# Windowed attention, low-rank mixing and a two-layer network in one kernel: mixing in 64-row halves, and one batch's attention two slots later

## The chip, the cores and the metric

The kernel runs on one core of a Trainium2 chip. The metric is device time in microseconds (us) of a whole execution, lower is better. A core has TensorE (matmuls, with a weight load before each), VectorE, ScalarE and GpSimd, and SyncE, which here only issues transfers. "DMA" is a transfer by the core's DMA engines. PSUM is the memory that matmuls write, divided into banks; SBUF is the other on-chip memory. The granted clock is the share of its full clock that TensorE was allowed, as the profile records it.

## The reference, cut to what matters

```python
# 8 batches, 8 heads, 576 positions, 64 values per head
scores = q @ k.T / sqrt(64)            # causal, window of 64
x = softmax(scores) @ v                # laid out as [batch, 576, 512]
h = (x.T @ U @ V).T                    # U: 576 x 32, V: 32 x 576: mixing along positions
u = x + h
out = u + relu(u @ w_ch1) @ w_ch2      # 512 -> 2048 -> 512
```

The 8 x 576 = 4608 rows are 36 tiles of 128. The network works in nine chunks of four tiles. A batch is four and a half tiles, so batch 3 covers tiles 13 (half of it) to 17, and chunk 3 (tiles 12 to 15) needs the first three of those.

## The kernel before

Everything is placed by hand. Chunk c of the network is 32 "fills" of four 128x512 matmuls each: 16 fills of the first layer (`psA`), then 16 of the second (`psU`, four for each tile). After fill s, the work listed for slot s is put into the program: in chunk c that is attention and mixing of batch c+1. In these traces each engine takes its matmuls, additions or transfers in program order, so "slot" fixes both when work runs and what it stands behind.

```python
PLACE = {"S": [0, 0, 0, 3, 3],   # scores
         "M": [0, 1, 2, 4, 5],   # masks
         "PV": [8],              # probabilities times values -> x
         "U": [14],              # down-product x.T @ U
         "V": [16, 17, 18],      # up-product, and u = x + h
         "UT": [17, 17, 18, 18, 19]}   # transposes of u
PLACE_3 = {**PLACE, "SV": [5, 5, 6, 6]}
...
for fill, extra in zip(mlp(c) + [lambda: None], slots):
    fill()
    for f in extra:
        f()
```

The down-product keeps four partial sums, one for each of the first four row tiles, in four groups of 32 PSUM partitions; the fifth tile is added to all four, 128 columns to each. The up-product contracts all 128 rows with V repeated four times:

```python
def UM(ts):                                  # down-product
    ...
        if t < 4:
            nc.tensor.matmul(hh["ps"][t * R : (t + 1) * R, :], ub[odd][:, t, :], xt,
                             start=True, stop=False)
            continue
        for g in range(4):
            cols = slice(g * P, (g + 1) * P)
            nc.tensor.matmul(hh["ps"][g * R : (g + 1) * R, cols], ub[odd][:, t, :],
                             xt[:, cols], start=False, stop=True)
    ...
def VM(ts):                                  # up-product and addition
    ...
        for n, t in enumerate(ts):
            off = t * P + (0 if odd else W)
            nc.tensor.matmul(ps[0][:, n, :], vrep[:, off : off + P], hh["sb"][:],
                             start=True, stop=True)
    ...                                      # add(n): u = psv + x, on VectorE
def UT(t):
    ...
        if b >= NXT:                         # batches 3 to 7: transposed by DMA
            nc.sync.dma_start_transpose(out=dst, in_=u_tiles[g][:])
            return
```

The last fill of each tile adds u and stores the result, through the same SyncE that issues the transposes:

```python
def ch2(t, quarter, ...):
    ...
        osb = out_pool.tile([P, DM], FP32, name="osb")
        nc.vector.tensor_tensor(out=osb[...], in0=acc[t][...], in1=u_tiles[g][...], op=ALU.add)
        nc.sync.dma_start(out=outf[...], in_=osb[...])
```

So tile 0 of a chunk is stored within slot 19's fill.

The softmax here doesn't subtract the row's maximum and nothing guards it: scores larger than these inputs give would overflow.

Of the kernel before, what the change touches and what calls it, by code (L numbers as in the profile page):

```python
# [12 lines left out]
FP32 = mybir.dt.float32  # L13
# [3 lines left out]
def kernel(  # L17
# [11 lines left out]
    nc = tc.nc  # L29
    B, H, S, D = q.shape  # L30
    DM = H * D
    R = moe_U.shape[1]
    F = moe_w_ch1.shape[1]
    P = nc.NUM_PARTITIONS
    W = 64
# [11 lines left out]
    CH = 512  # L47
# [17 lines left out]
    ps_big = ctx.enter_context(tc.tile_pool(name="ps_big", bufs=2, space=bass.MemoryType.PSUM))  # L65
    ps_tp = ctx.enter_context(tc.tile_pool(name="ps_tp", bufs=1, space=bass.MemoryType.PSUM))
    first = ExitStack()
    psum = {
        "spare": first.enter_context(tc.tile_pool(name="ps_s0", bufs=1, space=bass.MemoryType.PSUM)),
        "mm": first.enter_context(tc.tile_pool(name="ps_t0", bufs=2, space=bass.MemoryType.PSUM)),  # L70
    }
# [9 lines left out]
    NT = 5  # L81
    uf = [const.tile([P, NT, R], FP32, name=f"uf{i}") for i in range(2)]
    ub = [const.tile([P, NT, R], BF16, name=f"ub{i}") for i in range(2)]
    vrep = const.tile([P, W + S + W], BF16, name="vrep")
# [62 lines left out]
    def shift_low(b, copy, t):  # L147
# [9 lines left out]
        out=ident[:],  # L157
# [11 lines left out]
    for n, base, step, mult in ((0, 0, 1, -1), (1, -1, -1, 1), (1, W, 1, -1)):  # L169
        nc.gpsimd.affine_select(  # L170
            out=maskA[:, 0, n, :],
# [18 lines left out]
    for i in range(2):  # L190
# [5 lines left out]
        out=uf[0][:, 0:NFULL, :], in_=moe_U[0 : NFULL * P, :].rearrange("(c p) r -> p c r", p=P)  # L196
# [43 lines left out]
    u_tiles = {}  # L240
    uT_tiles = {}

    def uT_of(c):
        if c not in uT_tiles:
            uT_tiles[c] = uT_pool.tile([P, TPC, NDC, P], BF16, name="uTc")
        return uT_tiles[c]


    def attention(b, spare=False):
        crossbar = b >= NXB  # L250
        odd = b % 2
        kb, qb = staged(b)
        va, vb = vA[odd], vB[odd]
        x = xs[odd]
        g0 = (b * S) // P
        pcs = {}
# [231 lines left out]
        hh = {}  # L488
        xc = lambda src, t, dc: src[:, t, :, :].rearrange("p h d -> p (h d)")[:, dc * P : (dc + 1) * P]

        def UM(ts):
            def f():
                if ts[0] == 0:
                    if spare:
                        hh["ps"] = psum["spare"].tile([P, CH], FP32, name="psh", tag="spare")
                    else:
                        hh["ps"] = ps_big.tile([P, 2, CH], FP32, name="pshh", tag="big")[:, 0, :]
                for t in ts:
                    xt = x[:, t, :, :].rearrange("p h d -> p (h d)")
                    if t < 4:  # L500
                        nc.tensor.matmul(  # L501
                            hh["ps"][t * R : (t + 1) * R, :], ub[odd][:, t, :], xt,
                            start=True, stop=False,
                        )
                        continue

                    for g in range(4):
                        cols = slice(g * P, (g + 1) * P)
                        nc.tensor.matmul(
                            hh["ps"][g * R : (g + 1) * R, cols], ub[odd][:, t, :], xt[:, cols],  # L510
                            start=False, stop=True,
                        )
                if ts[-1] == NT - 1:
                    hh["sb"] = wk_pool.tile([P, CH], BF16, name="hh", tag="hh")
                    for cs in (slice(0, CH // 2), slice(CH // 2, CH)) if spare else (slice(0, CH),):
                        nc.scalar.copy(out=hh["sb"][:, cs], in_=hh["ps"][:, cs])
            return f
# [5 lines left out]
        def bank(dc):  # L523
            if dc not in ua:
                if dc < 2:
                    ua[dc] = psum["mm"].tile([P, CH], FP32, name="uam", tag="mm")[:]
                elif dc == 2:
                    ua[dc] = ps_tp.tile([P, CH], FP32, name="uat", tag="tp")[:]
                else:
                    ua[dc] = ps_big.tile([P, 2, CH], FP32, name="uab", tag="big")[:, 0, :]  # L530
            return ua[dc]
# [15 lines left out]
        def XT(t, dcs):  # L547
            def f():
                opened.append(t)
                for dc in dcs:  # L550
                    cols = bank(dc)[:, t * P : (t + 1) * P]

                    nc.tensor.matmul(cols, xc(x, t, dc), ident[:], start=(t == 0), stop=False)
            return f

        def HT(dcs):
            def f():
                for dc in dcs:
                    nc.tensor.matmul(
                        bank(dc),  # L560
                        hh["sb"][:, dc * P : (dc + 1) * P],
                        vrep[:, W : W + CH],
                        start=False,
                        stop=True,
                    )
                for dc in dcs:
                    copy = nc.scalar.copy if dc % 2 == 0 else nc.vector.tensor_copy
                    copy(
                        out=uT_of(b)[:, :, dc, :],
                        in_=bank(dc).rearrange("p (t q) -> p t q", q=P),  # L570
                    )
            return f

        def VM(ts):
            ps = {}

            def up():
                ps[0] = ps_big.tile([P, 2, CH], FP32, name="psv", tag="big")
                for n, t in enumerate(ts):
                    off = t * P + (0 if odd else W)  # L580
                    nc.tensor.matmul(  # L581
                        ps[0][:, n, :], vrep[:, off : off + P], hh["sb"][:], start=True, stop=True
                    )

            def add(n):
                def f():
                    t = ts[n]
                    g = g0 + t
                    rs = slice(
                        W if (odd and t == 0) else 0, W if (not odd and t == NT - 1) else P  # L590
                    )
                    if g not in u_tiles:
                        u_tiles[g] = u_pool.tile([P, DM], BF16, name="un")
                    nc.vector.tensor_tensor(  # L594
                        out=u_tiles[g][rs, :],
                        in0=ps[0][rs, n, :],
                        in1=x[rs, t, :, :].rearrange("p h d -> p (h d)"),
                        op=ALU.add,
                    )
                return f  # L600

            return [up] + [add(n) for n in range(len(ts))]

        def UT(t):
            def f():
                g = g0 + t
                dst = uT_of(g // TPC)[:, g % TPC, :, :]
                if b >= NXT:
                    nc.sync.dma_start_transpose(out=dst, in_=u_tiles[g][:])
                    return  # L610
                tp = ps_tp.tile([P, NDC, P], BF16, name="tpu", tag="tp")
                for dc in range(NDC):
                    nc.tensor.transpose(  # L613
                        tp[:, dc, :], u_tiles[g][:, dc * P : (dc + 1) * P], ident[:]
                    )
                nc.scalar.copy(out=dst, in_=tp[:])  # L616
            return f
# [13 lines left out]
        if spare:  # L631
            pcs["XT"] = [XT(t, range(NDC - 1)) for t in range(NFULL)]
            pcs["idle"] = idle_turns
            pcs["X3"] = [XT(t, (NDC - 1,)) for t in range(NFULL)]
            pcs["HT"] = [HT((0, 1)), HT((2, 3))]
            pcs["V"] = [f for ts in ((0, 1), (2, 3), (4,)) for f in VM(ts)]
        else:
            def whole(ts):
                fs = VM(ts)
                return lambda: [f() for f in fs]  # L640

            pcs["V"] = [whole(ts) for ts in ((0, 1), (2, 3), (4,))]
            pcs["UT"] = [UT(t) for t in range(NT if odd else NT - 1)]
        return pcs

# [4 lines left out]
    def mlp(c):  # L650
# [65 lines left out]
    PLACE = {  # L716
        "S": [0, 0, 0, 3, 3],
        "M": [0, 1, 2, 4, 5],
        "PV": [8],
        "U": [14],  # L720
        "V": [16, 17, 18],
        "UT": [17, 17, 18, 18, 19],
    }
    PLACE_0 = {"V": [0, 0, 1, 2, 2, 3, 4, 4]}
    PLACE_1 = {
        "T": [11, 11, 12, 12, 14, 14, 15, 15],
        "S": [12, 13, 15, 16, 16],
# [1 line left out]
        "SV": [17, 17, 18, 18],  # L729
        "PV": [19],  # L730
        "U": [24],
        "V": [25, 26, 27],
        "UT": [27, 28, 29, 30, 102],
    }
    PLACE_2 = {
# [2 lines left out]
        "SV": [15, 15, 16, 16],  # L738
        "PV": [18],
        "U": [23],  # L740
        "V": [24, 25, 26],
        "UT": [27, 28, 29, 30],
    }
    PLACE_3 = {**PLACE, "SV": [5, 5, 6, 6]}
    CROSS = {
        0: {2: [16, 17, 18, 19, 20]},
        1: {3: [13, 14, 15, 16, 17], 4: [26, 27, 28, 29, 30]},
# [7 lines left out]
    def turn_over(n, cols, rows=P):  # L755
# [5 lines left out]

    turn_over(62, 96)
    att = {0: attention(0, spare=True)}
    a = att[0]
    nc.vector.tensor_scalar(
        out=maskA[:, 0, 2, :],
        in0=maskA[:, 0, 1, :],
# [6 lines left out]
        out=maskB[:, 0:3, :],  # L774
        in0=maskA[:, 0, 0:3, :],
# [52 lines left out]
    for c in range(NCH):  # L828
# [10 lines left out]
        if b < B:  # L839
# [17 lines left out]
            if 2 < b and b + 2 < B:  # L857
                loads(b, 2)
            where = {1: PLACE_1, 2: PLACE_2, 3: PLACE_3}.get(b, PLACE)
            if b < NXB:  # L860
                place(b, ("T",), where)
            if b == 1:
                place(0, ("V",), PLACE_0)
                slots[6].append(lambda: nc.scalar.copy(out=ub[1][:], in_=uf[1][:]))
# [57 lines left out]
```

## Time and profile before

314.01 us, median of 3 runs (313.83 to 314.18).

The profiled execution was a separate one and took 315.07 us, 1 us more than the median.

| what | number | where read |
|---|---|---|
| span, TensorE busy | 313.4 us, 306.1 us | the page |
| start to start of 128x512 matmuls | 0.216 us | timeline |
| a middle chunk | 32.10 us | scores of batch 4 at 127.42, of batch 5 at 159.52 |
| wait before batch 3's scores | 1.07 us | timeline |
| third transpose of batch 3 landed, and was used | 126.24, 126.47 us | trace, timeline |

First the page: busy time of each engine with its share, then in 40 slices of the span the tenths that TensorE was busy and its granted clock in tenths.

```profile
...
PE 306.1 (98%) x2875; PEld 150.9 (48%) x2875; DVE 162.2 (52%) x298; ACT 108.6 (35%) x174; POOL 101.3 (32%) x133
...
PE   8899999999998999999999999999999999999996
...
PEclk9999999999999999999999999999999999999999
...
```

TensorE is busy in practically every slice at full clock. "Busy" alone would not prove that it is the limit, because reported ends of matmuls are modelled (0.379 us for one, though one starts every 0.216). The chain of waits does: each line is a start, a length and what the end of the kernel was waiting for in that stretch.

```profile
...
89.60 5.37 DMA qf<-qr
...
95.11 0.19 PE low L340
...
99.17 4.42 PE psA L663 x20
...
115.41 11.22 PE psU L687 x52
126.63 0.86 PE psA L663 x4
...
137.20 5.29 PE psA L663 x24
...
```

The transfer in the first line is the one that matters: TensorE waited for its end. The timeline of TensorE at this place (start, length, line, names, shapes, count, and in brackets the idle time before and what ended it):

```profile
...
93.08 1.03 PE L663 MATMUL psA<-uTc,w1b 128*128 128x512 bf16 x4
95.11 0.19 PE L340 MATMUL low<-qf,kf 64*64 64x64 bf16 x1 [1.00 <-DMA qf<-qr]
...
```

The fourth of those `psA` matmuls starts at 93.73, the score matmul 1.383 us later. In other chunks the same step takes 0.309 us, so 1.07 us are lost. The transposed queries landed at 94.98.

The queue of SyncE with VectorE and the mixing, where batch 3's u tiles are made (chunk 2):

```profile
...
112.44 0.59 PE L581 MATMUL psv<-hh,vrep 128*128 128x512 bf16 x2
...
113.07 3.21 DVE L594 TENSOR_TENSOR un<-psv,xs 64x512 bf16<-64x512 f32 x5 [3.88 <-PE psv L581]
...
114.19 0.53 SPq L703 DMA_DIRECT2D out_dram<-osb  x1
...
114.82 6.63 SPq L609 DMA_TRANSPOSE uTc<-un  x4
...
116.31 0.69 DVE L697 TENSOR_TENSOR osb<-psU,un 128x512 f32<-128x512 f32 x1
...
```

The transposes (`uTc<-un`) issue from 114.82 on; the third of them was issued at 117.54 and landed at 126.24. The store of tile 0, whose addition is the `osb` line at 116.31, comes after them. TensorE then goes into chunk 3 without a wait (no bracket at its first `psA`):

```profile
...
123.66 2.97 PE L687 MATMUL psU<-w2b,c 128*128 128x512 bf16 x13
...
126.47 1.03 PE L663 MATMUL psA<-uTc,w1b 128*128 128x512 bf16 x4
...
```

### The profile page before, as it was taken

How to read it: one execution, taken by the hardware profiler on the slowest of the kernel's cores; microseconds unless marked ns; L12 is line 12 of the kernel's file. 1: busy time of each engine (PE TensorE's matmuls, PEld its weight loads, DVE VectorE, ACT ScalarE, POOL GpSimd, SP SyncE). 2: the span in 40 equal slices, each digit the busy share in tenths (PEclk: the TensorE clock that was granted, in tenths of full speed). 3: DMA queues.
4: the chain of work that ended last, by engine and by line, in shares of the span. 5: the costliest groups of instructions: out<-in, count | busy, mean ns of one | idle time of the engine just before them, and what ended most of it. 6: DMA issues, size and time to landing. Idle time of an engine off the chain costs nothing.

```text
span 313.4 us, 6904 instructions
## 1 busy us (share of the span) xinstructions
PE 306.1 (98%) x2875; PEld 150.9 (48%) x2875; DVE 162.2 (52%) x298; ACT 108.6 (35%) x174; POOL 101.3 (32%) x133
## 2 busy tenths in 40 slices
PE   8899999999998999999999999999999999999996
PEld 7554554544444544454445444544454444444443
DVE  4475468337756843684358445744574443016011
ACT  3655660467027520533043404440345003301500
POOL 8683263159439346426543571000000000000000
PEclk9999999999999999999999999999999999999999
DMA  7999999999999999999999999965100520020012
GB/s 104 164 208 208 206 168 146 129 180 192 121 153 200 159 152 147 193 140 159 175 174 156 170 156 158 178 99 131 67 2 2 134 84 2 14 86 33 2 61 73
DMA packets 156495, 39.87 MB, mean 127 GB/s; under 512 B 145040, under 2 KB 151440, under 8 KB 156464
## 3 DMA queue, kind: packets, MB, share of 16 engines
q0 software_dynamic: 104720, 18.88, 82.5%
q1 hardware_dynamic: 51744, 20.55, 39.2%
q8 instruction: 22, 0.36, 0.4%
q14 instruction: 9, 0.07, 0.1%
HBM read 37.97 MB, written 9.44 MB: 151 GB/s over the span
## 4 chain that ended last, share of the span: by engine, by line
PE 81%; DMA 13%; POOL 3%; DVE 2%; issue 1%; SPq 0%; POOLq 0%
PE psU L687 36%; PE psA L663 36%; DMA qr<-in_q_dram 4%; DMA vB<-in_v_dram 4%; DMA vA<-in_v_dram 3%; PE psv L581 2%; PE xw L402 2%; PE sc L340 2%; DMA qf<-qr 2%; DVE xs L469 1%; POOL vA L134 1%; PE pshh L501 1%; POOL kr L116 1%; PE tpu L613 0%; POOL vrep L220 0%
## 5 line engine op out<-in xcount | busy, mean ns | idle before, releaser
L687 PE MATMUL psU<-w2b,c 128*128 128x512 bf16 (+2 forms) x592 | 131.3, 373 | 0.1
L663 PE MATMUL psA<-uTc,w1b 128*128 128x512 bf16 x576 | 131.0, 379 | 0.0
L687 PEld LDWEIGHTS <-c 128*128 128x128 bf16 x592 | 56.6, 98 | 64.8 <-issue 0.5
L663 PEld LDWEIGHTS <-w1b 128*128 128x128 bf16 x576 | 54.2, 98 | 64.4 <-issue 1.8
L675 ACT ACTIVATE c<-psA 128x512 bf16<-128x512 f32 x84 | 50.1, 597 | 88.8 <-PE psA L663 88.2
L697 DVE TENSOR_TENSOR osb<-psU,un 128x512 f32<-128x512 f32 (+2 forms) x37 | 24.9, 677 | 76.7 <-PE psU L687 76.3
L673 DVE TENSOR_SCALAR c<-psA 128x512 bf16<-128x512 f32 x60 | 41.3, 689 | 25.5 <-PE psA L663 25.5
L594 DVE TENSOR_TENSOR un<-psv,xs 128x512 bf16<-128x512 f32 (+1 forms) x40 | 25.5, 685 | 22.9 <-PE psv L581 22.7
L134 POOL DMA_DIRECT2D vA<-in_v_dram x32 | 28.6, 909 | 17.3 <-PE psU L687 3.1
L360 ACT ACTIVATE pts<-sc 128x1024 bf16<-128x1024 f32 x32 | 31.3, 1028 | 2.7 <-PE sc L340 2.7
L125 POOL DMA_DIRECT2D kr<-in_k_dram x30 | 25.8, 860 | 10.1 <-DMA vA<-in_v_dram 3.5
L125 POOL DMA_DIRECT2D qr<-in_q_dram x30 | 25.9, 864 | 8.9 <-DMA w2b<-in_moe_w_ch_dram 3.2
L393 ACT ACTIVATE ptl<-low 128x256 bf16<-128x256 f32 x6 | 2.3, 384 | 64.4 <-PE high L340 64.4
L366 DVE TENSOR_TENSOR pts<-pts,maskA 128x1024 bf16<-128x1024 bf16 x28 | 19.1, 682 | 1.1 <-ACT pts L360 1.1
L469 DVE TENSOR_TENSOR xs<-xw,rcw 128x896 bf16<-128x896 f32 x14 | 15.3, 1092 | 0.5
L340 PEld LDWEIGHTS <-kf 64*64 64x64 bf16 x704 | 9.9, 107 | 8.8 <-issue 8.2
L846 POOL COPY held<-qf 1x1 bf16<-1x1 bf16 x6 | 1.1, 178 | 39.4 <-DMA qf<-qr 39.4
L581 PE MATMUL psv<-hh,vrep 128*128 128x512 bf16 x40 | 12.5, 379 | 0.0
L402 PEld LDWEIGHTS <-pts 128*64 128x64 bf16 x512 | 10.0, 110 | 4.7 <-issue 3.7
L340 PE MATMUL sc<-qf,kf 64*64 64x128 bf16 (+1 forms) x608 | 11.6, 212 | 0.6 <-DVE qf L293 0.6
L134 POOL DMA_DIRECT2D vB<-in_v_dram x8 | 7.2, 901 | 5.9 <-DMA qr<-in_q_dram 2.5
L616 ACT COPY uTc<-tpu 128x512 bf16<-128x512 bf16 x9 | 5.3, 586 | 10.8 <-PE tpu L613 10.8
(108 smaller groups left out, 171.2 us busy)
## 6 DMA issues: line engine op xcount, KB each, us to landing
out_dram<-osb SPq DMA_DIRECT2D x35, 256.0 KB, 5.0
vA<-in_v_dram POOLq DMA_DIRECT2D x32, 128.0 KB, 13.1
kr<-in_k_dram POOLq DMA_DIRECT2D x24, 128.0 KB, 8.7
qr<-in_q_dram POOLq DMA_DIRECT2D x24, 128.0 KB, 8.9
w2b<-in_moe_w_ch_dram POOLq DMA_DIRECT2D x4, 512.0 KB, 15.7
vB<-in_v_dram POOLq DMA_DIRECT2D x8, 128.0 KB, 13.7
w1b<-in_moe_w_ch_dram POOLq DMA_DIRECT2D x2, 512.0 KB, 10.9
w1b<-in_moe_w_ch_dram POOLq DMA_DIRECT2D x1, 1024.0 KB, 10.0
```

Source lines behind the costliest of these rows:

```text
L125: nc.gpsimd.dma_start(out=dst[0:rows, t, :, :], in_=src[b, :, t * P : t * P + rows, :].rearrange("h p d -> p h d"),)
L134: nc.gpsimd.dma_start(out=dst[:, :, 0:D], in_=v[b, :, lo : lo + P, :].rearrange("h p d -> p h d"))
L340: nc.tensor.matmul(sc[g][r0 : r0 + W, col * W : (col + n) * W], keys_of(j, u, rs), queries_of(j, blk, n, rs), start=not spare, stop=last o ...
L360: nc.scalar.activation(out=dst, in_=sc[:], func=ACT.Exp, scale=scale)
L366: nc.vector.tensor_tensor(out=dst, in0=dst, in1=maskA.rearrange("p g n w -> p g (n w)"), op=ALU.mult)
L581: nc.tensor.matmul(ps[0][:, n, :], vrep[:, off : off + P], hh["sb"][:], start=True, stop=True)
L594: nc.vector.tensor_tensor(out=u_tiles[g][rs, :], in0=ps[0][rs, n, :], in1=x[rs, t, :, :].rearrange("p h d -> p (h d)"), op=ALU.add,)
L663: nc.tensor.matmul(ps[i][:], w1b[:, dc, i * P : (i + 1) * P], uTc[:, :, dc, :], start=(dc == 0), stop=(dc == NDC - 1),)
L673: nc.vector.tensor_relu(out=c1[i][:], in_=ps[i][:])
L675: nc.scalar.activation(out=c1[i][:], in_=ps[i][:], func=ACT.Relu)
L687: nc.tensor.matmul(acc[t][:, lo:hi], c1[i][:, t * P : (t + 1) * P], w2b[:, i, lo:hi], start=(i == 0), stop=(i == NFC - 1),)
L697: nc.vector.tensor_tensor(out=osb[:, lo:hi], in0=acc[t][:, lo:hi], in1=u_tiles[g][:, lo:hi], op=ALU.add,)
```

## The change: its intent and its diff

Two partial sums instead of four let the up-product contract 64 rows, so that two of its matmuls fit on the array side by side and run together. The price is that each row tile of the down-product is multiplied into two groups. All up-products of a batch move into one slot, with two more PSUM banks borrowed for the fifth tile. Batch 3's part of chunk 2 moves two slots later, to cover the wait for its queries.

```diff
 # down-product
-                        nc.tensor.matmul(
-                            hh["ps"][t * R : (t + 1) * R, :], ub[odd][:, t, :], xt,
-                            start=True, stop=False,
-                        )
+                        for g in (t % 2, t % 2 + 2):
+                            nc.tensor.matmul(
+                                hh["ps"][g * R : (g + 1) * R, :], ub[odd][:, t, :], xt,
+                                start=(t < 2), stop=False,
+                            )
...
-                        cols = slice(g * P, (g + 1) * P)
+                        cols = slice((g % 2) * CH // 2, (g % 2 + 1) * CH // 2)
 # up-product; HT, the first one of batch 0, is halved in the same way
-                for n, t in enumerate(ts):
-                    off = t * P + (0 if odd else W)
+                for n in range(2):
+                    half = slice(n * 2 * R, (n + 1) * 2 * R)
+                    off = ts[n % len(ts)] * P + (0 if odd else W)
+                    lo = 0 if len(ts) == 2 else n * cols
                     nc.tensor.matmul(
-                        ps[0][:, n, :], vrep[:, off : off + P], hh["sb"][:], start=True, stop=True
+                        ps[0][n], vrep[half, off : off + P], hh["sb"][half, lo : lo + cols],
+                        start=True, stop=True,
                     )
...
+            def mixed():
+                parts = [VM((0, 1)), VM((2, 3)), VM((NT - 1,), two_banks)]
+                for part in parts:
+                    part[0]()
+                for part in parts[2:] + parts[:2]:
+                    for add in part[1:]:
+                        add()
...
-        "V": [16, 17, 18],
+        "V": [16],
...
-    PLACE_3 = {**PLACE, "SV": [5, 5, 6, 6]}
+    PLACE_3 = {part: [s + 2 for s in at] for part, at in PLACE.items()}
+    PLACE_3["SV"] = [7, 7, 8, 8]
```

With "+2", batch 3's up-product stands at slot 18 and its transposes at 19, 19, 20, 20, 21.

More of the change, by code (lines that the diff above doesn't have):

```diff
@@ L557, in f @@
             def f():
-                for dc in dcs:
+                for n, dc in enumerate(dcs):
+                    half = slice(n * 2 * R, (n + 1) * 2 * R)
                     nc.tensor.matmul(
                         bank(dc),
-                        hh["sb"][:, dc * P : (dc + 1) * P],
-                        vrep[:, W : W + CH],
+                        hh["sb"][half, dc * P : (dc + 1) * P],
+                        vrep[half, W : W + CH],
                         start=False,
@@ L572, in HT, with VM @@
             return f
-        def VM(ts):
+        def VM(ts, banks=None):
             ps = {}
+            cols = CH if len(ts) == 2 else CH // 2
             def up():
-                ps[0] = ps_big.tile([P, 2, CH], FP32, name="psv", tag="big")
-                for n, t in enumerate(ts):
-                    off = t * P + (0 if odd else W)
+                if banks is None:
+                    pair = ps_big.tile([P, 2, CH], FP32, name="psv", tag="big")
+                    ps[0] = [pair[:, n, 0:cols] for n in range(2)]
+                else:
+                    ps[0] = [one[:, 0:cols] for one in banks()]
+                for n in range(2):
+                    half = slice(n * 2 * R, (n + 1) * 2 * R)
+                    off = ts[n % len(ts)] * P + (0 if odd else W)
+                    lo = 0 if len(ts) == 2 else n * cols
                     nc.tensor.matmul(
-                        ps[0][:, n, :], vrep[:, off : off + P], hh["sb"][:], start=True, stop=True
+                        ps[0][n], vrep[half, off : off + P], hh["sb"][half, lo : lo + cols],
+                        start=True, stop=True,
                     )
@@ L586, in f @@
                 def f():
-                    t = ts[n]
+                    t = ts[n % len(ts)]
                     g = g0 + t
@@ L591, in f @@
                     )
+                    cs = slice(0, CH) if len(ts) == 2 else slice(n * cols, (n + 1) * cols)
                     if g not in u_tiles:
@@ L594, in f @@
                     nc.vector.tensor_tensor(
-                        out=u_tiles[g][rs, :],
-                        in0=ps[0][rs, n, :],
-                        in1=x[rs, t, :, :].rearrange("p h d -> p (h d)"),
+                        out=u_tiles[g][rs, cs],
+                        in0=ps[0][n][rs],
+                        in1=x[rs, t, :, :].rearrange("p h d -> p (h d)")[:, cs],
                         op=ALU.add,
@@ L600, in add @@
                 return f
-            return [up] + [add(n) for n in range(len(ts))]
+            return [up, add(0), add(1)]
         def UT(t):
@@ L637, in attention, with two_banks @@
         else:
-            def whole(ts):
-                fs = VM(ts)
-                return lambda: [f() for f in fs]
-            pcs["V"] = [whole(ts) for ts in ((0, 1), (2, 3), (4,))]
+            def two_banks():
+                return (
+                    psum["mm"].tile([P, CH], FP32, name="psv0", tag="mm"),
+                    ps_tp.tile([P, CH], FP32, name="psv1", tag="tp"),
+                )
+            def mixed():
[5 more added lines that the diff above has]
+                        add()
+            pcs["V"] = [mixed]
             pcs["UT"] = [UT(t) for t in range(NT if odd else NT - 1)]
@@ L720 @@
         "U": [14],
-        "V": [16, 17, 18],
+        "V": [16],
         "UT": [17, 17, 18, 18, 19],
     }
-    PLACE_0 = {"V": [0, 0, 1, 2, 2, 3, 4, 4]}
+    PLACE_0 = {"V": [0, 0, 1, 2, 2, 3, 4, 4, 4]}
     PLACE_1 = {
@@ L731 @@
         "U": [24],
-        "V": [25, 26, 27],
+        "V": [25],
         "UT": [27, 28, 29, 30, 102],
@@ L740 @@
         "U": [23],
-        "V": [24, 25, 26],
+        "V": [24],
         "UT": [27, 28, 29, 30],
     }
-    PLACE_3 = {**PLACE, "SV": [5, 5, 6, 6]}
+    PLACE_3 = {part: [s + 2 for s in at] for part, at in PLACE.items()}
+    PLACE_3["SV"] = [7, 7, 8, 8]
     CROSS = {
```

## The prediction

> **What bounds it.** TensorE: the page gives it 306.1 of 313.4 us busy at full clock, and from 130 us on the chain of waits is TensorE almost without a break. In the timeline 128x512 matmuls start every 0.216 us; a middle chunk repeats every 32.10 us (127.49, 159.59). The one sizeable idle stretch after the start is at 95.11 us: batch 3's first score matmul waits for transposed queries (landed 94.98). It starts 1.383 us after the matmul before it; elsewhere that step takes 0.309, so 1.07 us are lost.
>
> **What the change does to TensorE**, from start-to-start times:
> - Up-product now: five matmuls, 5 x 0.216 = 1.08 us per batch, no cost at their edges. After: two pairs of 64-row halves of 512 columns and one of 256. If a pair runs concurrently (the Trainium skill, "TensorE: Matmul & The Clock Gate", Part 3, says that matmuls on different row groups do; in this trace the four 32-column matmuls of the down-product start 3 ns apart), that is 0.54 us. But partial-array blocks pay at their edges here: 0.309 instead of 0.216 on entry, about 0.10 more on exit. Estimate 0.74: saves 0.34.
> - Down-product: each row tile goes to two column groups, so two rounds of 0.216 instead of one, and the last tile streams 256 columns, not 128: +0.27.
> - Net about -0.07 per batch, -0.5 us in all; in batch 0 nothing, as copies follow its first up-product.
> - Two slots (1.73 us) cover batch 3's 1.07 us wait; perhaps 0.15 returns, because ScalarE's exponentials now precede a ReLU.
>
> **What it breaks.** Chunk 3's first matmul needs batch 3's first three u tiles, transposed by DMA. Now the third is issued at 117.54 and lands at 126.24; that matmul starts at 126.47: 0.2 us of slack. After, batch 3's mixing stands at slot 18, at about T = 113.3 us; its own 0.74 and 13 fills of 0.863 bring TensorE to chunk 3 at T+12.0 = 125.3. The transposes come later: all six additions are one run on VectorE (estimate: end T+4.25), and slot 19's output store now precedes them in the DMA queue, waiting for an addition behind that run (T+4.9). So they issue at about T+5.6, 6.9, 8.3, and the third lands, with 7.7 us as measured around 122, near 129.3. TensorE would wait about 4 us (1.5 to 5.5). Such a wait may also lower the clock (same page, Part 1; no run here shows it yet). Other chunks need only two tiles, placed ahead of the store: no wait.
>
> **Sum**: 314.0 - 0.5 - 1.07 + 0.15 + 4 = 316.6; allowing for a shorter or missing wait, 316.0 us, range 312.2 to 318.6. Chances: faster by over 2% 0.01, within 2% 0.95, slower by over 2% 0.04.
>
> **What would show it.** (1) Psv pairs starting a few ns apart, the block about 0.74 us. (2) The pshh block 0.27 us longer. (3) No DMA wait before batch 3's scores. (4) A TensorE wait of about 4 us on uTc at the first psA of chunk 3, near 125 us, and an output store ahead of the uTc transposes in the DMA queue. (5) Middle chunks near 32.03 us.
>
> **What would make it wrong.** Halves that do not overlap (+0.5 us per batch). Transposes landing faster, or issued before the store: then about 312.5. Clock loss after the wait: 318 or more. PSUM banks borrowed for the last part delaying the next chunk.

## The result, and the profile after

318.62 us, median of 6 runs (316.16 to 319.34), against 314.1 us (313.63 to 314.52) in the same rounds. The ratio is 1.013, 95% interval 1.0092 to 1.0168: slower, but by less than 2%. Ratios here and below are the mean time of one kernel's runs over that of the other's in the same rounds, so not quite the ratio of the medians.

The page after:

```profile
...
PE 306.5 (97%) x2915; PEld 148.7 (47%) x2915; DVE 162.7 (51%) x306; ACT 109.1 (34%) x174; POOL 101.2 (32%) x133
...
PE   8889999999999998799999999999999999999996
...
PEclk9999999999999999799999999999999999999999
...
```

In the sixteenth and seventeenth slices (118.7 to 134.5 us) TensorE is no longer full, and in the second of them its clock is at 0.7. The chain of waits shows what stands before it:

```profile
...
113.11 0.69 PE psv L590 x6
...
114.13 0.41 DVE un L605
...
115.27 1.89 DVE un L605 x3
117.15 0.61 DVE osb L718
117.78 0.34 SPq L724
118.16 1.30 SPq L620
119.52 1.43 SPq L620
120.99 7.08 DMA uTc<-un
128.21 1.31 PE psA L684 x4
...
```

Read downwards: up-product of batch 3 (113.11), its six additions (to 117.15), the addition for tile 0's output (117.15), its store (SPq, the queue of SyncE, 117.78), the transposes of u (118.16, 119.52), the third one's landing (120.99 to 128.08), and only then the first `psA` of chunk 3. The same stretch in the timeline, as shown for the kernel before:

```profile
...
113.04 0.71 PE L590 MATMUL psv<-hh,vrep 64*128 64x512 bf16 x6
...
113.79 3.36 DVE L605 TENSOR_TENSOR un<-psv,xs 128x256 bf16<-128x256 f32 x6 [4.36 <-PE psv L590]
113.83 4.29 SPq L724 DMA_DIRECT2D out_dram<-osb  x2
...
117.07 0.68 DVE L718 TENSOR_TENSOR osb<-psU,un 128x512 f32<-128x512 f32 x1
...
118.16 4.15 SPq L620 DMA_TRANSPOSE uTc<-un  x3
...
```

The store line at 113.83 merges two: that of chunk 1's last tile, and the one that waited for the addition at 117.07. Before, three of the transposes had been issued by 118.9. TensorE at the start of chunk 3:

```profile
...
123.63 1.46 PE L708 MATMUL psU<-w2b,c 128*128 128x512 bf16 x6
128.21 1.31 PE L684 MATMUL psA<-uTc,w1b 128*128 128x512 bf16 x4 [3.13 <-DMA uTc<-un]
...
```

From start to start, 3.505 us lie between the last `psU` and this `psA` instead of 0.216: a wait of 3.29 us. The wait before batch 3's scores is gone: they start 0.309 us after the matmul before them.

The wait is not all. Busy time of each engine, its instructions, the granted clock (third number from the end), DMA share and GB/s in three stretches: chunk 2, 3 and 4 of the changed kernel, each from its first `psA` to the next chunk's.

```profile
...
92.88:128.21 35.33, 32.21 (x307) 14.90 (x306) 20.73 (x37) 11.85 (x19) 20.99 (x26) 1.00 1.86 166
128.21:161.79 33.58, 33.58 (x306) 15.61 (x307) 17.91 (x32) 10.28 (x16) 15.23 (x19) 0.95 1.81 165
161.79:193.84 32.05, 32.05 (x308) 14.99 (x307) 18.55 (x33) 10.28 (x16) 12.92 (x16) 1.00 1.92 171
...
```

Chunk 3 takes 33.58 us and chunk 4, with the same work, 32.05. In chunk 3 four `psA` matmuls still start 0.215 to 0.244 us apart after the wait; then the clock falls to a half (0.50 from 128.85 to 132.20): the score matmuls that follow are slowed too, the next `psA`, from 130.66 to 132.29, start 0.37 to 0.43 us apart, and after that 0.216 again. Chunk 3 loses 1.5 us to it (33.58 less 32.05).

The mixing itself, for batch 4, before and after:

```profile
...
142.41 0.40 PE L501 MATMUL pshh<-xs,ub 128*32 128x512 bf16 x4
...
144.54 0.59 PE L581 MATMUL psv<-hh,vrep 128*128 128x512 bf16 x2
...
```

```profile
...
145.69 0.61 PE L502 MATMUL pshh<-xs,ub 128*32 128x512 bf16 x8
...
148.18 0.71 PE L590 MATMUL psv<-hh,vrep 64*128 64x512 bf16 x6
...
```

The six matmuls of the new up-product start in pairs 3 to 4 ns apart. From the last matmul on the full array to the next such one, less one ordinary step, the block takes 0.742 us instead of five steps of 0.216 (1.08). The down-product takes 0.75 instead of 0.48. A middle chunk takes 32.04 or 32.05 us instead of 32.10.

Where the profiled executions differ (spans of 316.43 and 313.37 us), from the starts of the chunks' first `psA`:

| stretch | before | after | difference |
|---|---|---|---|
| to the first psA | 21.97 | 22.41 | +0.44 |
| chunk 0 | 37.89 | 37.31 | -0.58 |
| chunk 1 | 33.22 | 33.16 | -0.06 |
| chunk 2 | 33.39 | 35.33 | +1.94 |
| chunk 3 | 32.10 | 33.58 | +1.48 |
| the rest | 154.80 | 154.64 | -0.16 |

Of the first line, 0.38 us is the arrival of the first queries, which differs from execution to execution. Of chunk 0, about 0.5 us is a wait for batch 1's values that this execution of the kernel before had and another one with the same mixing (e2 below, 37.41 us) had not. Chunk 2 is 3.29 of new wait, 1.07 of vanished wait, 0.2 that is lost no more in batch 3's values product and what follows it (from its first matmul to the down-product 6.79 us before, 6.58 after), and 0.07 of mixing.

The two profiles are 3.06 us apart, the times 4.1 (by the ratio) to 4.5 us (by the medians). The profiled execution of the kernel before was 1 us slower than its median, and three of the six of the changed kernel took 319.09 to 319.34 us, about 1 us more than its profiled one (318.14 us). Those three were not traced, so where their further microsecond went is not known.

### The profile page after: what moved, and what is told of

Read it like the earlier page. It is cut to its first block, busy times and chain, and to the rows that moved or that the text cites. A ratio compares the mean times of both kernels' runs of the same rounds, so it can differ in the third digit from the quotient of the medians.

```text
span 316.4 us, 6992 instructions
## 1 busy us (share of the span) xinstructions
PE 306.5 (97%) x2915; PEld 148.7 (47%) x2915; DVE 162.7 (51%) x306; ACT 109.1 (34%) x174; POOL 101.2 (32%) x133
## 4 chain that ended last, share of the span: by engine, by line
PE 90%; DMA 4%; DVE 2%; SPq 1%; ACT 1%; issue 1%; POOL 0%; POOLq 0%
PE psA L684 41%; PE psU L708 36%; PE sc L340 3%; PE xw L402 2%; DMA uTc<-un 2%; DMA qr<-in_q_dram 2%; PE psv L590 2%; PE pshh L502 1%; SPq L620 1%; DVE un L605 1%; PE tpu L624 1%; ACT pts L360 1%; PE tpg L276 1%; PE xr L402 1%; DVE qf L293 0%
## 5 line engine op out<-in xcount | busy, mean ns | idle before, releaser
L708 PE MATMUL psU<-w2b,c 128*128 128x512 bf16 (+2 forms) x592 | 129.4, 374 | 0.0
L708 PEld LDWEIGHTS <-c 128*128 128x128 bf16 x592 | 55.9, 98 | 65.5 <-issue 3.2
L605 DVE TENSOR_TENSOR un<-psv,xs 128x512 bf16<-128x512 f32 (+3 forms) x48 | 26.1, 592 | 26.0 <-PE psv L590 25.8
L517 ACT CAST hh<-pshh 128x512 bf16<-128x512 f32 x7 | 4.1, 585 | 13.6 <-PE pshh L510 13.5
```

The source lines that it names most:

```text
L605: nc.vector.tensor_tensor(out=u_tiles[g][rs, cs], in0=ps[0][n][rs], in1=x[rs, t, :, :].rearrange("p h d -> p (h d)")[:, cs], op=ALU.add,)
L708: nc.tensor.matmul(acc[t][:, lo:hi], c1[i][:, t * P : (t + 1) * P], w2b[:, i, lo:hi], start=(i == 0), stop=(i == NFC - 1),)
```

## The experiments

Nine kernels, in three calls (e1 to e4; e5 to e7; e8 and e9), each call on another chip and each kernel with five timed rounds beside the kernel before. All gave correct results. Batch 3's third transpose ("third UT") is the one that chunk 3 needs last; all columns are of the one profiled execution, times in us:

| run | wait before batch 3's scores | third UT issued | landed | wait at chunk 3 | chunk 3 | from first psA to the end |
|---|---|---|---|---|---|---|
| before | 1.07 | 117.54 | 126.24 | 0 | 32.10 | 291.40 |
| changed | 0 | 120.99 | 128.08 | 3.29 | 33.58 | 294.02 |
| e1 new mixing alone | 0.63 | 118.54 | 125.15 | 0 | 32.04 | 290.38 |
| e2 shift alone | 0 | 118.66 | 126.74 | 2.33 | 32.09 | 291.96 |
| e3 transposes first | 0 | 118.59 | 125.64 | 1.10 | 32.04 | 290.42 |
| e4 and additions in order | 0 | 117.72 | 124.67 | 0.03 | 32.04 | 289.46 |
| e5 changed, loads later | 0 | 120.43 | 124.09 | 0 | 32.04 | 289.19 |
| e6 changed, filler | 0 | 121.00 | 129.27 | 1.59 after 3.0 of filler | 32.04 | 293.80 |
| e7 e4 and loads later | 0 | 119.27 | 121.75 | 0 | 32.04 | 289.20 |
| e8 old mixing, in order | 0 | 116.99 | 124.76 | 0 | 32.10 | 290.47 |
| e9 e4 again | 0 | 120.14 | 128.13 | 0.07 | 32.04 | 289.26 |

The last column leaves out the start, which differs by 0.4 us and more between executions for reasons that have nothing to do with the change.

The theory: the mixing is nearly neutral; the shift takes away one wait and makes another, because the store of slot 19 comes to stand ahead of batch 3's transposes in SyncE's queue and itself waits for the run of six additions. Rivals: the mixing costs the time; the shift alone costs it, whatever the order; the clock, not the wait, is the loss.

### e1: the new mixing alone

```diff
-    PLACE_3 = {part: [s + 2 for s in at] for part, at in PLACE.items()}
-    PLACE_3["SV"] = [7, 7, 8, 8]
+    PLACE_3 = {**PLACE, "SV": [5, 5, 6, 6]}
```

> The new mixing alone, batch 3 at its old slots. Theory (the output store that moved ahead of the transposes in the DMA queue makes the loss; the mixing itself is nearly neutral): the 1.07 us wait for queries before batch 3's scores is back, transposes of batch 3's u tiles issue before the store from about 114.5 us, the wait at the first psA of chunk 3 is 0 to 1 us, no clock loss; 313.6 to 314.6 us, ratio 0.999 to 1.002. Rival (the mixing costs the time: burst of additions, borrowed PSUM banks): 316 us or more.

Measured: 314.4 us median (313.46 to 316.53), the kernel before 314.34; ratio 1.0015 (0.9986 to 1.0044). No wait at chunk 3, clock 1.0, and the transposes stand before the store again:

```profile
...
114.68 6.48 SPq L620 DMA_TRANSPOSE uTc<-un  x4
121.25 0.53 SPq L724 DMA_DIRECT2D out_dram<-osb  x1
...
```

So the mixing does not make the loss. Two of the six executions, at 315.72 and 316.53 us with a clock of 1.0, were slower for a reason that was not traced. Whether the mixing earns its 0.05 us per batch can't be seen in the times, only in the length of the chunks.

### e2: the shift alone, with the old mixing

```diff
-    PLACE_3 = {**PLACE, "SV": [5, 5, 6, 6]}
+    PLACE_3 = {part: [s + 2 for s in at] for part, at in PLACE.items()}
+    PLACE_3["SV"] = [7, 7, 8, 8]
```

> The old mixing, batch 3 two slots later alone. Theory: the store of slot 19 stands ahead of the transposes here too, but the store's addition follows only two of the five additions, so the third transpose issues near 118.5 instead of 121.0 us: no wait before batch 3's scores, a wait of 1 to 2.5 us at the first psA of chunk 3; 314 to 315.5 us. Rival (the loss needs no burst, the shift alone makes all of it): 317 us or more with a wait of over 3 us.

Measured: 315.95 us (315.48 to 318.28); ratio 1.0065 (1.0037 to 1.0093). The third transpose issued at 118.66 and landed at 126.74, and TensorE waited:

```profile
...
PE psA L663 <- DMA uTc<-un: 2.2, 1, 2.2
...
```

Transposes, wait and mechanism are as the theory had them (2.33 us from start to start); the time is above its range. Two of the six executions, at 316.96 and 318.28 us, had a granted clock of 0.994 and 0.995, which the expectation left out. So the shift makes a loss with either mixing. With the new one the store, behind all six additions, lets the third transpose go 2.3 us later still (120.99), and the wait is 1 us longer.

### e3: batch 3's transposes ahead of the store

```diff
+    PLACE_3["UT"] = [18, 18, 18, 19, 19]
```

> The changed kernel, with batch 3's first three transposes issued in slot 18, before the store of slot 19. Theory (the order in the queue costs most): the third transpose issues near 118.3 instead of 121.0 us, the wait at chunk 3 falls from 3.3 to 0.5 to 1.5 us, little or no clock loss; about 314 to 315 us. Rival (two slots later is too late whatever the order, because landing takes 7 us or more and TensorE needs 12 us): the wait stays over 2.5 us and the time over 317.

Measured: 314.39 us (313.75 to 315.32); ratio 1.0006 (0.9986 to 1.0026). The order in the queue, nothing else, was changed:

```profile
...
115.05 4.77 SPq L620 DMA_TRANSPOSE uTc<-un  x3
119.92 0.65 SPq L724 DMA_DIRECT2D out_dram<-osb  x1
...
```

The wait fell from 3.29 to 1.10 us and the clock stayed at 1.0. This takes back nearly all of the loss. Against the rival: two slots later is not too late as such.

### e4: and the additions in the order of the tiles

```diff
-                for part in parts[2:] + parts[:2]:
+                for part in parts if b == 3 else parts[2:] + parts[:2]:
```

> As the run before, and batch 3's additions in the order of its tiles, so that the last tile's two halves no longer stand first (0.85 us on VectorE). Theory: the third transpose issues another 0.8 us earlier, near 117.4, wait 0 to 0.7 us, 313 to 314 us, at best just under the kernel before. Rival (the DMA queue, not VectorE, is the limit by then): same as the run before within 0.3 us.

Measured: 313.43 us (313.19 to 314.25); ratio 0.9977 (0.9958 to 0.9996).

```profile
...
114.12 4.84 SPq L620 DMA_TRANSPOSE uTc<-un  x3
...
```

The third transpose issued at 117.72, 0.9 us earlier than in e3, and landed at 124.67; the `psA` that needs it started at 124.81, 0.03 us late. So VectorE's order was still a limit, and with both mendings the wait is gone. The time is 0.2% under the kernel before, less than intended: the prediction put a version whose transposes issue before the store near 312.5 us.

### e6: TensorE kept busy through the wait

Fourteen matmuls of zeros into a free PSUM bank after chunk 2's last fill, on the changed kernel.

```diff
+        if c == 2:
+            def filler():
+                fill_ps = ps_tp.tile([P, CH], FP32, name="filler", tag="tp")
+                for _ in range(14):
+                    nc.tensor.matmul(fill_ps[:], idle[:, 0:P], idle[:], start=True, stop=True)
+            slots[31].append(filler)
```

> The changed kernel with 14 matmuls of zeros (3.0 us) put on TensorE between chunk 2 and the first psA of chunk 3, so that it does not stand idle while it waits for the transposes. Theory (the idle wait itself lowers the clock, which costs about 1 us more after it): the remaining wait is 0.2 to 1 us, no matmul after it takes 0.43 us from start to start, the granted clock is 1.0, and the time is 0.8 to 1.5 us below that of the changed kernel in its own runs: about 317. Rival (the clock falls for another reason, or the spread of the changed kernel, 316.2 to 319.3 us, comes from elsewhere): the half-rate matmuls stay and the time is that of the changed kernel.

Measured: 316.98 us (316.14 to 317.78); ratio 1.0087 (1.0063 to 1.0112), against the changed kernel's 1.013 (1.0092 to 1.0168) in its own rounds. The granted clock was 1.0 in all six executions; the changed kernel had 0.994 or 0.995 in five of six, and the sixth, at 0.999, was its fastest (316.16 us).

```profile
...
124.79 3.19 PE L915 MATMUL filler<-idle 128*128 128x512 bf16 x14
129.41 1.02 PE L684 MATMUL psA<-uTc,w1b 128*128 128x512 bf16 x4 [1.43 <-DMA uTc<-un]
...
```

After a filler of 3.0 us and a wait of 1.59, chunk 3 takes 32.04 us, not 33.58. In this execution the third transpose landed 1.2 us later than in the changed kernel's, so the wait left was longer than expected (0.2 to 1 us). So the idle time lowers the clock, and that costs 1.5 us where it happens; the length of chunk 3 and the clocks of the twelve executions show this. In the times it would be about a third of the loss (the ratios differ by 0.0043, or 1.35 us), but the two intervals overlap, so the times alone do not show it. It is no remedy: the wait itself stays.

### e5: fewer loads under way while u is transposed

GpSimd issues batch 5's key and query loads once a given tile of batch 4's transposed queries is there. On the changed kernel:

```diff
-                loads(b, 2)
+                loads(b, NT - 1 if b == 3 else 2)
```

> The changed kernel, but batch 5's key and query loads wait for batch 4's last transposed tile instead of its third, some 6 us later (119 instead of 113.5 us), so that fewer loads are under way when batch 3's u tiles are transposed. The order in the store's queue stays bad: third transpose issued near 121. Theory (landing takes 7 us because those loads share the DMA engines): landing falls to 3 to 5.5 us and the wait at chunk 3 from 3.3 to 0 to 1.8 us; 314 to 316 us. Rival (landing is a fixed cost of the transpose): landing stays over 6.5 us, the wait over 2.5 us, 317 us or more.

Measured: 314.47 us (313.15 to 315.2); ratio 1.0006 (0.9981 to 1.0031). Three transposes with their median time from issue to landing, in the changed kernel:

```profile
...
uTc<-un SPq DMA_TRANSPOSE x3, 7.3
```

and in this run, where the loads began at 120.85 instead of 114.29 us:

```profile
...
uTc<-un SPq DMA_TRANSPOSE x3, 3.7
```

Although the third transpose was issued nearly as late as in the changed kernel (120.43 against 120.99), it landed at 124.09, and there was no wait at chunk 3. So the transposes' 7 us are not theirs: the loads hold them up. The Trainium skill ("DMA: Bandwidth & Descriptors", section "Issuing engines are not separate DMA queues") says that transfers issued by different engines run on the same DMA engines and interleave; this agrees, 7.3 against 3.7 us. The profiled execution was the fastest of the six. What the others, up to 315.2 us at a clock of 1.0, waited for was not traced.

### e7: order and loads together

The edits of e3, e4 and e5.

> The changed kernel with all three mendings: transposes before the store, additions in the order of the tiles, batch 5's loads later. The run with the first two had the third transpose landing 0.1 us before its use, so theory: no wait at chunk 3 with some us to spare, 312.8 to 313.6 us and a smaller spread, no later wait for batch 5's queries. Rival (the later loads only move the wait to batch 5's scores in chunk 4): 314 us or more, with a wait of DMA near 158 us.

Measured: 313.17 us (312.86 to 316.55); ratio 0.9997 (0.9959 to 1.0035), wide because of one execution at 316.55 us with a clock of 0.989. The third transpose landed at 121.75, 2.7 us before its use, and no wait for batch 5's queries appeared. The same trace repeats what e5 showed: the loads begin at 120.29; the third transpose, issued at 119.27, took 2.5 us to land, the fifth, issued at 122.47 among the loads, 7.2. Four of six executions are at 313.25 us or less. Whether this beats e4 is not decided by these rounds.

### e8 and e9: which part earns the gain

e8 is the kernel before with the shift, its old mixing and the transposes first; e9 is e4 once more, beside it.

```diff
 # e8, on the kernel before with the shift
+    PLACE_3["V"] = [18, 18, 19]
+    PLACE_3["UT"] = [18, 18, 18, 19, 19]
```

> The old mixing (128-row up-products) with batch 3 two slots later, its up-products at slots 18, 18, 19 and its first three transposes in slot 18, ahead of the store. Theory (the whole gain of the mended version is the vanished wait for queries, the new mixing adds 0.05 us per batch and can hardly be seen): no wait before batch 3's scores, 0 to 0.7 us at chunk 3, middle chunks of 32.10 us, 313.2 to 314.2 us, within 0.6 us of the mended version with the new mixing run beside it. Rival (the new mixing earns the gain): 314.3 us or more, as the kernel before.

> The mended version (transposes before the store, additions in the order of the tiles) once more, beside the one with the old mixing: middle chunks of 32.05 us, ratio to the kernel before again 0.996 to 0.9995, about 313.4 us. If the first result was luck: a ratio of 1.000 or more.

Measured: e8 314.28 us (313.87 to 316.47), ratio 1.0007 (0.9973 to 1.0042); e9 313.88 us (312.84 to 316.65), ratio 0.998 (0.9945 to 1.0015). The medians are 0.4 us apart, the intervals overlap: the times don't settle it, and e8 lies a little above its range, at the edge of its rival's (314.3). e9 repeats e4's 0.2%, but its interval includes 1, so that gain is not clear of noise. The profiles say more. e8 has middle chunks of 32.10 us, and before the fifth tile's up-product TensorE waits 0.4 us for an addition, which has to free a PSUM bank: the old mixing borrows none. Chunk 0 took it 37.86 us, against 37.31 to 37.55 with the new mixing, again with a wait for batch 1's values, which is no part of the mixing.

The profiled execution of e9 was its slowest, and shows where this one's time went. The tenths of the granted clock of e9 and e4:

```profile
...
PEclk9969999999999999999999999999999999999999
...
```

```profile
...
PEclk9999999999999999999999999999999999999999
...
```

In e9 batch 0's first queries were late:

```profile
...
13.41 0.45 PE L276 MATMUL tpg<-ident,qr 96*64 96x96 bf16 x12 [1.66 <-DMA qr<-in_q_dram]
...
```

Its first `psA` starts at 25.69 us instead of 22.03, and from there to the end it takes 289.26 us, less than e4's 289.46. The kernel before had an execution with the same clock in the same rounds (316.6 us at 0.989; another took 316.42 us at 0.995; neither was traced), so such a start is probably no part of the change. Slow executions at a clock of 1.0, as in e1, have another cause, which was not looked for.

## Why the prediction was right, and where its sizes were off

- **Direction, mechanism and place were right.** Slower by under 2%; the one large new wait is TensorE's, on the third transpose, at the first `psA` of chunk 3; a store ahead of the transposes, behind six additions. Predicted issue times 118.9, 120.2, 121.6 us with T = 113.3; measured 118.16, 119.52, 120.99 with T = 113.04. e3 and e4 show the two orders to be the cause: with both undone the wait is 0.03 us.
- **The wait was a little too large**: 4 us predicted, 3.29 measured in the profiled execution. Landing took 7.1 us, not 7.7, and the issue was 0.6 us earlier; TensorE, too, came to chunk 3 0.4 us earlier (124.92 instead of 125.3), which gave 0.4 us of that back.
- **The clock was left out of the sum.** The prediction named it only as a way to be wrong ("318 or more"). It happened in five of six executions; chunk 3 measured 1.5 us more for it, and e6, which keeps TensorE busy, lost nothing to it. This is the mis-sized term: 0 in the sum, 1.5 us measured. The Trainium skill ("TensorE: Matmul & The Clock Gate", section "Why this matters for your kernels") warns of idle gaps of more than about 3 us between bursts of matmuls; the 3.29 us gap of this trace agrees. These runs give no threshold, though: e2's gap of 2.33 us left chunk 3 at 32.09 us in its profile, while in e9's start the clock fell to a half at 14.72 us after an idle stretch of only 1.66 us, with shorter ones around it.
- **The discount was wrong.** From a sum of 316.6 us the prediction went down to 316.0 "for a shorter or missing wait". The median, 318.62 us, is 2.6 us above that and 0.02 above the upper end of the stated range; by the ratio (314.1 x 1.013 = 318.2) it is just inside. The two sizes that were off, a wait put 0.7 us too large and a clock loss of 1.5 us left out, partly cancel in the sum; that is luck.
- **The mixing was right, to a few hundredths**: block 0.742 us (predicted 0.74), down-product +0.27 (predicted +0.27), net 0.05 to 0.06 us per batch (predicted 0.07), nothing gained in the first up-product of batch 0. The matmuls of a pair do overlap (starts 3 to 4 ns apart), as the Trainium skill states ("TensorE: Matmul & The Clock Gate", Part 3). What eats the gain are the edges, the steps from full-array matmuls into the block and out of it: 0.311 us instead of 0.216 on entry, and about 0.10 on exit. The Trainium skill ("TensorEngine Tiling (Array Packing)", Key Properties) says that a change of tiling mode drains the engine; the trace agrees in that both edges cost time, 0.2 us per block here, but no run separates a drain from another cause.
- **The old wait went as predicted**: 1.07 us, and 0.2 more behind it in batch 3's values product. The 0.15 us that ScalarE was to give back did not appear.
- **What stays open**: whether the new mixing is worth having at all in time (0.4 us between e8 and e9 is within the noise), what the slower half of e5's executions waited for, and why three of the changed kernel's six executions took about 1 us more than its profiled execution.

## What to carry to other kernels

Before moving a block later, look at what its results feed and how long before their use they arrive: here 0.2 us of slack lay behind the wait that was being removed. In a queue that issues in program order, moving work by two slots can put it behind a store that waits for something else; keep the transfers that the critical engine needs ahead of those that nobody waits for, and order the additions by who is waiting. Halving a small matmul to run it in pairs pays only what is left after its edges, so count them in the trace first.

## What the Trainium skill lacked or had wrong

- "TensorEngine Tiling (Array Packing)", Key Properties: a mode switch drains, but no cost is given. Here: 0.309 to 0.312 us from the last full matmul to the first partial one instead of 0.216, and about 0.10 us after the last; a block of 64-row pairs with 0.54 us of columns takes 0.742.
- "TensorE: Matmul & The Clock Gate", Back-to-back issue gap: it gives about 131 ns per matmul of 512 columns as the sustained rate of weight-load and matmul pairs. Here 64 such pairs in a row (the kernel before from 255.03 us on, in the chain of waits) take 13.81 us, 216 ns each; that is the figure it calls the isolated gap.
- The same page, Part 1, gives an idle window of about 3.4 us as what lowers the clock. Here 3.29 us of waiting was enough in the changed kernel, and 1.66 us with shorter idle stretches around it in e9. In the changed kernel the granted clock fell only 0.6 us after work had resumed; the half-rate steps ended 4.1 us after it, at a cost of 1.5 us.
- "DMA: Bandwidth & Descriptors", DMA Transpose: no landing time of a small transpose under load. Here, 128x512 of 2-byte values from SBUF to SBUF: medians of the first three of batch 3 are 8.7 us (before) and 7.3 us (changed) with loads of GpSimd's queue under way, 3.7 us (e5) and 3.1 us (e7) with fewer.
